# Both halves of a group's scores in one two-bank PSUM tile with a single exponential, in a one-token attention and MLP block

## The chip, the cores and the metric

The kernel runs on one core of a Trainium2 chip. A core has a matrix engine (TensorE, PE in the rows; its weight loads are PEld), a vector engine (VectorE, DVE), a scalar engine (ScalarE, ACT), GpSimd (POOL), and a queue processor (SyncE, SP) that issues the transfers from memory (DMA). TensorE writes only to PSUM, an accumulator of eight banks; a bank holds 512 fp32 columns in each of the 128 partitions. The working memory is SBUF. The metric is device microseconds of one execution, as the median of several. All data here is fp32.

## What is computed

One new token for each of four sequences passes through an attention over the last 1024 cached positions (8 groups of key and value heads, two query heads each) and then through an MLP, both behind a layer norm and with a residual:

```python
B, Sq, D = 4, 1, 448;  Hq, Hkv, Sk, Dh = 16, 8, 4096, 256
W = min(4096, max(256, Sk // 4))                     # 1024 positions
q = (x @ wq).reshape(B, Sq, Hq, Dh).transpose(0, 2, 1, 3)
k = jnp.repeat(k_cache[:, :, Sk - W:, :], rep, axis=1)
v = jnp.repeat(v_cache[:, :, Sk - W:, :], rep, axis=1)
scores = jnp.einsum("bhqd,bhkd->bhqk", q, k) * (Dh ** -0.5)
o = jnp.einsum("bhqk,bhkd->bhqd", softmax(scores), v)
...                                                   # o @ wo, back to (B, 1, D)
x = A_x
h = x + A(layernorm(x), A_k_cache, A_v_cache, A_wq, A_wo)
h2 = h + B(layernorm(h), B_w1, B_b1, B_w2, B_b2)      # B: layernorm, gelu(y @ w1 + b1) @ w2 + b2
```

Each input is read once: 88 MB of keys, values and weights, nearly all of it caches.

## The kernel before

**Groups.** The 8 groups of key and value heads (g = 0 to 7) are worked one after another. For one group the kernel projects the query (`project_q`, L149), multiplies it with the keys (`scores_half`, L168, once for each 512 of the 1024 positions), forms the softmax (`softmax`, L180), transposes the probabilities (`transpose_p`, L200), multiplies them with the values (`values`, L213), scales and transposes the result (`transposed_output`, L231) and multiplies it with the group's output weights into one accumulator (`add_output`, L243); the last two together are `finish` (L298). The steps of neighbouring groups are interleaved: while group g+1 has its scores formed, the values of group g are used.

**Transfers.** Keys, values and weights come in large packed transfers, one after another on SyncE's single queue (`load`, L54). They land in a ring of three SBUF slots of 15,872 columns (`slot`, L51). A transfer into a slot can only be issued when the last reader of what lay there before is done, for most slots the output product of a `finish`. The order is t0 (first weights and the keys of group 0), then twice ta, tb, tc and td (L302 to L332, for g = 0 and g = 3), then te0, te1 and te2 (L336 to L343), which hold the keys of group 7, the values and output weights of groups 6 and 7, and the MLP's weights `w1` and `w2`. The slots te are filled in pieces. Of `w2`, which is used last, pieces of 8, 3, 2 and 1 chunks come in this order.

**One group's softmax.** The two halves of the scores are two PSUM tiles of one bank each, from a pool with two buffers (`ps_s`, L43). After each half VectorE takes the row maximum over 512 columns (L177). Then two small VectorE operations form the larger of the two maxima and multiply it with minus the scale (L183 and L184), ScalarE runs one exponential for each half with that as its bias (L188), each with its own row sum, and VectorE adds the two sums and takes the reciprocal (L193, L194). `transpose_p` has TensorE transpose four blocks of 128 columns for each half (L204); the first four read only the first half of the probabilities. In groups 3 and 6 the two halves of the keys come in different transfers (tc and td), and other work lies between the two halves (L318 to L326). In the other six groups the 16 matmuls of both halves follow each other directly (`scores`, L197).

**Order.** The order of TensorE, ScalarE and SyncE is the order of the program text; VectorE's and GpSimd's are set by a scheduler that puts in the waits too. Every engine works strictly in its order.

**The end.** After group 7's scores (L344) TensorE runs two matmuls whose result is not used (`fill`, L353), transposes group 7's probabilities, and goes on with the values of groups 6 and 7 and the MLP. Short matmuls on a zero tile (`keep_warm`, L349) stand in the gaps. The first eight chunks of `w2` are multiplied at L469, the others at L479, and the result is added at L485 and written out. Two other tiles come from the pool `ps_s`: `last` (L372) for the attention's output and `pu` (L430) for the MLP's first product.

**Rows at the start.** The token and the two biases are turned into rows by six transposes (L289), and ScalarE copies them from PSUM (L291).

Of the kernel before, what the change touches and what calls it, by code (L numbers as in the profile page):

```python
# [20 lines left out]
P = 128  # L21
# [4 lines left out]
FQ = F // 4  # L26
Q = 32
# [6 lines left out]
SCALE = DH ** -0.5  # L34

@with_exitstack
def block_kernel(ctx: ExitStack, tc, wq0, k0, wq1, la, lb, lc, ld, k7, vo, w1, w2, out):
    nc = tc.nc
    const = ctx.enter_context(tc.tile_pool(name="const", bufs=1))
    ring = ctx.enter_context(tc.tile_pool(name="ring", bufs=3))  # L40
    work = ctx.enter_context(tc.tile_pool(name="work", bufs=2))
    once = ctx.enter_context(tc.tile_pool(name="once", bufs=1))
    ps_s = ctx.enter_context(tc.tile_pool(name="ps_s", bufs=2, space=PSUM))  # L43
    ps_t = ctx.enter_context(tc.tile_pool(name="ps_t", bufs=2, space=PSUM))
    ps_o = ctx.enter_context(tc.tile_pool(name="ps_o", bufs=1, space=PSUM))
    ps_m = ctx.enter_context(tc.tile_pool(name="ps_m", bufs=2, space=PSUM))
# [32 lines left out]
    def keys(t):  # L79
        return t.rearrange("p (c b k) -> p c b k", c=2, b=B)  # L80
# [35 lines left out]
    qT = [const.tile([P, 2, B, Q], F32, name=f"qT{i}") for i in range(2)]  # L116
# [48 lines left out]
        for i in range(2):  # L165
            nc.vector.tensor_copy(qT[g % 2][:, :, :, i * REP : (i + 1) * REP], src)

    def scores_half(g, h, kt):  # L168
        s = ps_s.tile([P, 512], F32, tag="s", name=f"s{g}_{h}")
        for c in range(2):  # L170
            for b in range(B):
                nc.tensor.matmul(  # L172
                    s[b * Q : (b + 1) * Q, :], qT[g % 2][:, c, b, :], kt[:, c, b, :],
                    start=(c == 0), stop=(c == 1),
                )
        m = work.tile([P, 1], F32, tag=f"mx{h}", name=f"mx{g}_{h}")
        nc.vector.reduce_max(m, s, axis=AX.X)  # L177
        return s, m

    def softmax(g, parts):  # L180
        halves, mx = zip(*parts)
        nm = work.tile([P, 1], F32, tag="nm", name=f"nm{g}")
        nc.vector.tensor_max(nm, mx[0], mx[1])  # L183
        nc.vector.tensor_scalar_mul(nm, nm, -SCALE)  # L184
        p = once.tile([P, 2 * 512], F32, tag="p", name=f"p{g}")
        sums = work.tile([P, 2], F32, tag="sums", name=f"sums{g}")
        for h in range(2):
            nc.scalar.activation(  # L188
                p[:, h * 512 : (h + 1) * 512], halves[h], AF.Exp, bias=nm, scale=SCALE,
                accum_out=sums[:, h : h + 1],  # L190
            )
        rec = work.tile([P, 1], F32, tag=f"rec{g % 3}", name=f"rec{g}")
        nc.vector.tensor_add(rec, sums[:, 0:1], sums[:, 1:2])  # L193
        nc.vector.reciprocal(rec, rec)  # L194
        return p, rec

    def scores(g, kt):  # L197
        return [scores_half(g, h, kt[h]) for h in range(2)]

    def transpose_p(g, p):  # L200
        for h in range(2):
# [84 lines left out]
    for at, n in ((0, 2), (2 * P, 4)):  # L286
        pr = ps_t.tile([P, n, P], F32, tag="t", name=f"pr{n}")
        for i in range(n):
            nc.tensor.transpose(pr[:, i, :], wide[:, at // P + i].rearrange("p j q -> p (j q)"), ident)  # L289
        cols = min(n * P, rs.shape[1] - at)  # L290
        nc.scalar.copy(rs[:, at : at + cols], pr.rearrange("p i c -> p (i c)")[:, :cols])  # L291

    parts = scores(0, [keys(ka), keys(kb)])
    project_q(1, wq_parts(wqt1, wq1_last))
# [7 lines left out]
    for g in (0, 3):  # L302
        ka, kb, wqt, va = cut(load(slot(f"ta{g}"), 0, la[g // 3]), (HALF, HALF, WEIGHTS, HALF))
        parts = scores(g + 1, [keys(ka), keys(kb)])
        project_q(g + 2, wq_parts(wqt))
        p, rec_next = softmax(g + 1, parts)
        transpose_p(g + 1, p)
        po = po_tile(g)
        va = chunks(va)
        values(g, va, po, range(0, 2))  # L310

        vb, wot, ka, kb = cut(load(slot(f"tb{g}"), 0, lb[g // 3]), (HALF, WEIGHTS, HALF, HALF))
        values(g, va + chunks(vb), po, range(2, 4))
# [8 lines left out]
        first_half = scores_half(g + 3, 0, keys(ka))  # L322
# [3 lines left out]
        parts = [first_half, scores_half(g + 3, 1, keys(kb))]  # L326
        project_q(g + 4, wq_parts(wqt))
        p, rec = softmax(g + 3, parts)
# [40 lines left out]

    keep_warm(2, warm)  # L370
    values(g + 1, vt_last, po_last, range(0, 3))
    last = ps_s.tile([P, 512], F32, tag="s", name="last")[:, :P]  # L372
    ph = last.rearrange("p (i c) -> p i c", i=2)
    add_quadrants(ph, accs, True)
    values(g + 1, vt_last, po_last, range(3, 4))
# [181 lines left out]
```

## Time and profile before

| | |
|---|---|
| median of 3 runs | 213.93 us (213.82 to 213.99) |
| the profiled execution | 214.16 us, of which its span is 212.4 us |
| busy share of the span | PE 63%, PEld 23%, DVE 18%, ACT 10%, POOL 2% |
| the transfer queue's packets | 96.9% of 16 DMA engines over the span, 88.30 MB |
| mean rate over the span | 416 GB/s |
| granted TensorE clock, mean | 0.854 |

The span runs from the first to the last instruction of the profiled execution; the other 1.76 us of its time lie around it. No engine is busy for more than two thirds of the span, while the DMA engines are busy nearly all of it. The row of the granted clock on the page alternates between full and half speed:

```profile
PEclk9999995995896559589969759856985999999999
DMA  7999898999999999999999999999989999999991
```

A digit is a fortieth of the span, 5.3 us; under PEclk it is the clock in tenths, under DMA the busy share in tenths. Up to the thirty-first slice the clock falls to half again and again; after that it stays full.

### The profile page before, as it was taken

The numbers are of one execution on the slowest core, as the hardware profiler recorded it, in microseconds if no ns is written. First come the engines' busy times: TensorE is split into PE (matmuls) and PEld (weight loads), VectorE is DVE, ScalarE is ACT, GpSimd is POOL, SyncE is SP. The second block draws the span as 40 slices with busy tenths as digits, with TensorE's granted clock in tenths as the row PEclk, the third lists the DMA queues.
The fourth block names the chain that finished last, engine by engine and source line by source line (L and its number), as shares of the span: only waits on it lengthen the run. The fifth ranks groups of instructions, "written<-read, shape, count | busy, mean of one in ns | idle before, by whom it ended". The sixth has DMA issues, their size and how long they took to land.

```text
span 212.4 us, 2302 instructions
## 1 busy us (share of the span) xinstructions
PE 133.9 (63%) x976; PEld 48.3 (23%) x976; DVE 39.0 (18%) x170; ACT 22.1 (10%) x54; POOL 5.0 (2%) x16
## 2 busy tenths in 40 slices
PE   0469805843950696288398098138708879978984
PEld 0342201310220221022123023013202323224432
DVE  1520300410230003022013013100301223112310
ACT  2011300300020100030003002001000302010311
POOL 5100000000000000000000000000000000000200
PEclk9999995995896559589969759856985999999999
DMA  7999898999999999999999999999989999999991
GB/s 294 425 396 534 361 488 361 491 394 475 407 395 529 395 407 430 451 403 459 424 424 488 403 395 505 395 430 419 478 350 460 430 429 394 440 400 444 419 384 52
DMA packets 3257, 88.43 MB, mean 416 GB/s; under 512 B 368, under 2 KB 624, under 8 KB 1328
## 3 DMA queue, kind: packets, MB, share of 16 engines
q1 hardware_dynamic: 3248, 88.30, 96.9%
q8 instruction: 7, 0.11, 0.2%
q14 instruction: 2, 0.02, 0.0%
HBM read 88.23 MB, written 0.07 MB: 416 GB/s over the span
## 4 chain that ended last, share of the span: by engine, by line
DMA 78%; PE 16%; SPq 2%; DVE 1%; issue 1%; ACT 1%; ACTq 0%
DMA tb<-lb 22%; DMA ta<-la 21%; DMA td<-ld 20%; DMA te<-w 14%; PE s L172 6%; PE po L216 4%; SPq L58 2%; PE ppt L204 1%; PE pq L152 1%; PE acc L245 1%; PE pa L469 1%; PE py L479 1%; SPq L265 1%; PE pqt L158 1%; ACT qs L154 1%
## 5 line engine op out<-in xcount | busy, mean ns | idle before, releaser
L177 DVE TENSOR_REDUCE mx<-s 128x1 f32<-128x512 f32 x16 | 11.1, 691 | 57.8 <-PE s L172 57.8
L172 PE MATMUL s<-ta,qT 128*32 128x512 f32 x64 | 10.7, 831 | 10.3 <-DMA ta<-la 10.3
L154 ACT COPY qs<-pq 128x512 f32<-128x512 f32 x8 | 4.7, 585 | 113.3 <-PE pq L152 113.3
L188 ACT ACTIVATE p<-s,nm 128x512 f32<-128x512 f32 x16 | 10.9, 687 | 46.1 <-DVE nm L184 46.1
L233 DVE TENSOR_SCALAR o<-po,rec 128x512 f32<-128x512 f32 x8 | 6.0, 750 | 48.5 <-PE po L216 48.5
L216 PE MATMUL po<-tb,pT 128*32 128x512 f32 x32 | 7.2, 1051 | 12.2 <-DMA tb<-lb 12.2
L172 PE MATMUL s<-td,qT 128*32 128x512 f32 x32 | 7.1, 1042 | 12.1 <-DMA td<-ld 12.1
L152 PE MATMUL pq<-tc,yT 128*32 128x512 f32 (+1 forms) x20 | 3.9, 891 | 16.6 <-DMA tc<-lc 16.6
L204 PE MATMUL ppt<-ident,p 128*128 128x128 f32 x64 | 10.5, 287 | 0.7 <-ACT p L188 0.4
L216 PE MATMUL po<-tc,pT 128*32 128x512 f32 x64 | 10.4, 813 | 0.0
L158 PE MATMUL pqt<-ident,qs 128*128 128x128 f32 x32 | 6.6, 341 | 6.0 <-ACT qs L154 6.0
L204 PEld LDWEIGHTS ppt<-ident,p 128*128 128x128 f32 x64 | 6.7, 141 | 6.3 <-ACT p L188 6.3
L160 DVE TENSOR_REDUCE sm<-pqt 128x16 f32<-128x64 f32 x8 | 1.8, 224 | 34.4 <-PE pqt L158 34.4
L216 PE MATMUL po<-te,pT 128*32 128x512 f32 x64 | 7.5, 595 | 0.5 <-DMA te<-vo 0.5
L172 PE MATMUL s<-tb,qT 128*32 128x512 f32 x64 | 7.4, 607 | 0.0
L216 PE MATMUL po<-td,pT 128*32 128x512 f32 x64 | 7.3, 595 | 0.0
L237 PE MATMUL pot<-ident,o 128*128 128x128 f32 x32 | 5.2, 286 | 2.7 <-DVE o L233 2.7
L158 PEld LDWEIGHTS pqt<-ident,qs 128*128 128x128 f32 x32 | 4.2, 169 | 11.4 <-ACT qs L154 9.7
L351 PE MATMUL warm<-idle 128*32 128x512 bf16 x22 | 6.8, 382 | 0.0
L172 PEld LDWEIGHTS s<-ta,qT 128*32 128x32 f32 x64 | 2.6, 148 | 17.7 <-issue 13.7
L208 DVE COPY pT<-ppt 128x16 f32<-128x16 f32 x32 | 4.7, 171 | 7.6 <-PE ppt L204 7.6
L172 PE MATMUL s<-t,qT 128*32 128x512 f32 x32 | 5.4, 833 | 0.5 <-DMA t<-k 0.5
(134 smaller groups left out, 112.4 us busy)
## 6 DMA issues: line engine op xcount, KB each, us to landing
tc<-lc SPq DMA_DIRECT2D x2, 7936.0 KB, 47.0
td<-ld SPq DMA_DIRECT2D x2, 7936.0 KB, 44.0
ta<-la SPq DMA_DIRECT2D x2, 7040.0 KB, 38.1
tb<-lb SPq DMA_DIRECT2D x2, 7040.0 KB, 43.2
te<-vo SPq DMA_DIRECT2D x1, 4992.0 KB, 28.1
t<-k SPq DMA_DIRECT2D x1, 4864.0 KB, 15.8
te<-k SPq DMA_DIRECT2D x1, 4096.0 KB, 37.8
te<-vo SPq DMA_DIRECT2D x1, 3072.0 KB, 14.8
```

What stands on the lines that cost most here:

```text
L152: nc.tensor.matmul(pq[j * Q : (j + 1) * Q, cols], y, w, start=True, stop=True)
L154: nc.scalar.copy(qs, pq)
L158: nc.tensor.transpose(pt[:, i, :], qs[:, i * P : (i + 1) * P], ident)
L172: nc.tensor.matmul(s[b * Q : (b + 1) * Q, :], qT[g % 2][:, c, b, :], kt[:, c, b, :], start=(c == 0), stop=(c == 1),)
L177: nc.vector.reduce_max(m, s, axis=AX.X)
L188: nc.scalar.activation(p[:, h * 512 : (h + 1) * 512], halves[h], AF.Exp, bias=nm, scale=SCALE, accum_out=sums[:, h : h + 1],)
L204: nc.tensor.transpose(pt[:, c, :], p[:, (4 * h + c) * P : (4 * h + c + 1) * P], ident)
L208: nc.vector.tensor_copy(pT[g % 2][:, 2 * h : 2 * h + 2, :, i * REP : (i + 1) * REP], src[:, :, i, :, :REP])
L216: nc.tensor.matmul(po[b * Q : (b + 1) * Q], pT[g % 2][:, c, b, :], vt[c][:, :, b, :], start=(c == 0), stop=(c == NKC // 2 - 1),)
L233: nc.vector.tensor_scalar_mul(o, po, rec)
L237: nc.tensor.transpose(pt[:, i, c], o[:, i, c * P : (c + 1) * P], ident)
L351: nc.tensor.matmul(warm[:Q], idle[:, :Q], idle, start=True, stop=True)
```

## The change

The two halves of a group's scores become one PSUM tile of two banks, from a pool with one buffer instead of two of one bank, so the pool takes as much PSUM as before. The two row maxima go into the two columns of one small tile. One VectorE operation takes the larger of the two columns and multiplies it with minus the scale. One exponential runs over all 1024 columns and leaves the whole row sum, so the addition of two sums goes. The copies of the rows at the start move from ScalarE to VectorE. `last` and `pu` take the first bank of a two-bank tile.

```diff
-    ps_s = ctx.enter_context(tc.tile_pool(name="ps_s", bufs=2, space=PSUM))
+    ps_s = ctx.enter_context(tc.tile_pool(name="ps_s", bufs=1, space=PSUM))
...
-    def scores_half(g, h, kt):
-        s = ps_s.tile([P, 512], F32, tag="s", name=f"s{g}_{h}")
+    def score_tile(g):
+        s = ps_s.tile([P, 2, 512], F32, tag="s", name=f"s{g}")
+        return s, work.tile([P, 2], F32, tag="mx", name=f"mx{g}")
+
+    def scores_half(g, h, kt, part):
+        s, mx = part
         for c in range(2):
             for b in range(B):
                 nc.tensor.matmul(
-                    s[b * Q : (b + 1) * Q, :], qT[g % 2][:, c, b, :], kt[:, c, b, :],
+                    s[b * Q : (b + 1) * Q, h, :], qT[g % 2][:, c, b, :], kt[:, c, b, :],
                     start=(c == 0), stop=(c == 1),
                 )
-        m = work.tile([P, 1], F32, tag=f"mx{h}", name=f"mx{g}_{h}")
-        nc.vector.reduce_max(m, s, axis=AX.X)
-        return s, m
-
-    def softmax(g, parts):
-        halves, mx = zip(*parts)
+        nc.vector.reduce_max(mx[:, h : h + 1], s[:, h, :], axis=AX.X)
+
+    def softmax(g, part):
+        s, mx = part
         nm = work.tile([P, 1], F32, tag="nm", name=f"nm{g}")
-        nc.vector.tensor_max(nm, mx[0], mx[1])
-        nc.vector.tensor_scalar_mul(nm, nm, -SCALE)
+        nc.vector.tensor_scalar(nm, mx[:, 0:1], mx[:, 1:2], -SCALE, op0=ALU.max, op1=ALU.mult)
         p = once.tile([P, 2 * 512], F32, tag="p", name=f"p{g}")
-        sums = work.tile([P, 2], F32, tag="sums", name=f"sums{g}")
-        for h in range(2):
-            nc.scalar.activation(
-                p[:, h * 512 : (h + 1) * 512], halves[h], AF.Exp, bias=nm, scale=SCALE,
-                accum_out=sums[:, h : h + 1],
-            )
         rec = work.tile([P, 1], F32, tag=f"rec{g % 3}", name=f"rec{g}")
-        nc.vector.tensor_add(rec, sums[:, 0:1], sums[:, 1:2])
+        nc.scalar.activation(
+            p, s.rearrange("p h k -> p (h k)"), AF.Exp, bias=nm, scale=SCALE, accum_out=rec
+        )
         nc.vector.reciprocal(rec, rec)
         return p, rec
...
-        nc.scalar.copy(rs[:, at : at + cols], pr.rearrange("p i c -> p (i c)")[:, :cols])
+        nc.vector.tensor_copy(rs[:, at : at + cols], pr.rearrange("p i c -> p (i c)")[:, :cols])
...
-    last = ps_s.tile([P, 512], F32, tag="s", name="last")[:, :P]
+    last = ps_s.tile([P, 2, 512], F32, tag="s", name="last")[:, 0, :P]
...
-    pu = ps_s.tile([P, 512], F32, tag="s", name="pu")[:, :FQ]
+    pu = ps_s.tile([P, 2, 512], F32, tag="s", name="pu")[:, 0, :FQ]
```

The callers pass the tile along (`scores` for six groups, the loop over tc and td for groups 3 and 6) and are otherwise as before.

**TensorE, the scores of group 7.** Two pieces of the engine's order show what the text alone does not. Names are the program's tiles: `s` is the scores, `te` a ring slot (here the one with group 7's keys), `qT` the queries, `DVE_49` the count that VectorE's instructions raise, `DMAHW4_49` a transfer's. Before:

```order
L172 MATMUL s_0_835<-te_821,qT_112 32x512 [waits DMAHW4_49]
L172 MATMUL s_0_835<-te_821,qT_112 32x512 x7
L172 MATMUL s_1_846<-te_821,qT_112 32x512 x8
L355 MATMUL warm_867<-te_821,yT 32x512 x2
L204 MATMUL ppt_0_870<-ident,p_860 128x128 [waits Activation_49]
L204 MATMUL ppt_0_870<-ident,p_860 128x128 x3
L204 MATMUL ppt_1_877<-ident,p_860 128x128 [waits Activation_49]
```

With the change:

```order
L176 MATMUL s_793<-te_779,qT_112 32x512 [waits DMAHW4_49]
L176 MATMUL s_793<-te_779,qT_112 32x512 x7
L176 MATMUL s_793<-te_779,qT_112 32x512 [waits DVE_49]
L176 MATMUL s_793<-te_779,qT_112 32x512 x7
L356 MATMUL warm_819<-te_779,yT 32x512 [waits PE_49]
L356 MATMUL warm_819<-te_779,yT 32x512
L204 MATMUL ppt_0_822<-ident,p_815 128x128 [waits Activation_49]
L204 MATMUL ppt_0_822<-ident,p_815 128x128 x3
L204 MATMUL ppt_1_829<-ident,p_815 128x128 x4
```

The first matmul of the second half now waits for VectorE; the count that it waits for is that of the first half's maximum. All of the transposes now wait for one exponential. The same wait stands in groups 0, 1, 2, 4, 5 and 7. In groups 3 and 6, where other work lies between the halves, it does not:

```order
L176 MATMUL s_677<-tc_641,qT_111 32x512 [waits DVE_49]
L176 MATMUL s_677<-tc_641,qT_111 32x512 x7
L237 MATMUL pot_690<-ident,o_688 128x128 [waits DVE_49]
L237 MATMUL pot_690<-ident,o_688 128x128 x3
L245 MATMUL acc<-tc_641,oT_115 32x448 [waits DVE_49]
L245 MATMUL acc<-tc_641,oT_115 32x448 x3
L176 MATMUL s_677<-td_701,qT_111 32x512 [waits DMAHW3_49]
L176 MATMUL s_677<-td_701,qT_111 32x512 x7
```

These rows are group 6 with the change; the second half, from td, waits for its transfer alone.

**VectorE, group 0.** The copies of the rows (`rs`) now stand on VectorE, the first of them ahead of the copies of the queries, `qT`, that group 0's scores read:

```order
L160 TENSOR_REDUCE sm_168<-pqt_163 128x16 [waits PE_49]
L291 COPY rs<-pr_175 128x256 [waits PE_49]
L166 COPY qT_111<-sm_168 128x8x2 [waits DVE_49]
L166 COPY qT_111<-sm_168 128x8x2
L291 COPY rs<-pr_179 128x448 [waits PE_49]
L180 TENSOR_REDUCE mx_186<-s_185 128x1 [waits PE_49] x2
```

Before, the first copy of `qT` followed the reduction `sm` directly, and both copies of the rows stood on ScalarE between two copies of L154.

More of the change, by code (lines that the diff above doesn't have):

```diff
@@ L197, in scores @@
     def scores(g, kt):
-        return [scores_half(g, h, kt[h]) for h in range(2)]
+        part = score_tile(g)
+        for h in range(2):
+            scores_half(g, h, kt[h], part)
+        return part
     def transpose_p(g, p):
@@ L321, in block_kernel @@
         values(g + 1, chunks(v), po)
-        first_half = scores_half(g + 3, 0, keys(ka))
+        part = score_tile(g + 3)
+        scores_half(g + 3, 0, keys(ka), part)
         finish(g + 1, po, rec_next, wot)
         kb, wqt, v, wot = cut(load(slot(f"td{g}"), 0, ld[g // 3]), (HALF, WEIGHTS, CACHE, WEIGHTS))
-        parts = [first_half, scores_half(g + 3, 1, keys(kb))]
+        scores_half(g + 3, 1, keys(kb), part)
         project_q(g + 4, wq_parts(wqt))
-        p, rec = softmax(g + 3, parts)
+        p, rec = softmax(g + 3, part)
         transpose_p(g + 3, p)
```

## Prediction

> **What bounds the kernel now.** I read the page's chain of waits first, then the transfer queue, then the waits, and last the timeline of the final 50 us.
>
> ```profile
> DMA 78%; PE 16%; SPq 2%; DVE 1%; issue 1%; ACT 1%; ACTq 0%
> q1 hardware_dynamic: 3248, 88.30, 96.9%
> PE pq L152 <- DMA tc<-lc: 16.6, 2, 8.5
> PE po L216 <- DMA tb<-lb: 12.2, 2, 6.4
> PE s L172 <- DMA td<-ld: 12.1, 2, 6.7
> PE s L172 <- DMA ta<-la: 10.3, 2, 7.1
> ```
>
> The first row is the chain by engine: transfers make 78% of it. The second says that the queue's packets fill 96.9% of the DMA engines. The other four are waits (sum, times, longest): TensorE stands idle before every big transfer, and the shortest of these eight waits is 10.3 − 7.1 = 3.2 us. So up to td's second landing each stage starts with a landing, and what a stage computes late ends in that idle time, as long as it is below 3.2 us and the next transfer is still asked for early enough. The place where asking is tightest is te's:
>
> ```profile
> 174.13 1.28 SPq L58 DMA_DIRECT2D te<-vo  x3
> 181.70 0.19 PEld L216 LDWEIGHTS po<-te,pT 128*32 128x32 f32 x8 [0.75 <-PE warm L351]
> 181.73 3.64 PE L216 MATMUL po<-te,pT 128*32 128x512 f32 x32 [0.28 <-DMA te<-vo]
> 160.10 3.64 PE L172 MATMUL s<-td,qT 128*32 128x512 f32 x16 [6.71 <-DMA td<-ld]
> ```
>
> (start and duration in us, and in brackets the idle time and what ended it.) The second piece of `vo` is asked for at 174.13, while the first lands only just before 181.73: 7.5 us in hand. So the stream's end doesn't move with a delay of a microsecond or two. From 160.10, td's last landing, it is different: TensorE computes on to the end with four short waits for transfers, and that stretch, the tail, is where this change can be felt. I call a wait there slack: a delay is eaten by it.
>
> **Part 1: the exponential of group 6**, in the tail.
>
> ```profile
> 165.38 0.69 ACT L188 ACTIVATE p<-s,nm 128x512 f32<-128x512 f32 x1
> 165.96 0.20 ACT L188 ACTIVATION_READ_ACCUMULATOR p<-s,nm 128x1 f32 x1
> 166.21 0.42 PEld L204 LDWEIGHTS ppt<-ident,p 128*128 128x128 f32 x4 [0.26 <-ACT p L188]
> 166.22 1.32 PE L204 MATMUL ppt<-ident,p 128*128 128x128 f32 x8
> L188 ACT ACTIVATE p<-s,nm 128x512 f32<-128x512 f32 x16 | 10.9, 687 | 46.1 <-DVE nm L184 46.1
> L154 ACT COPY qs<-pq 128x512 f32<-128x512 f32 x8 | 4.7, 585 | 113.3 <-PE pq L152 113.3
> L291 ACT COPY rs<-pr 128x256 f32<-128x256 f32 x1 | 0.4, 372 | 1.7 <-PE pr L289 1.7
> ```
>
> The first transposes start 0.83 us after the first exponential (166.21 − 165.38), while the second is still running, and all eight then take 1.32 us without a gap. No row has a pass of 1024 columns. ScalarE's copies give the price of a column: (585 − 372)/256 = 0.83 ns, so 512 more cost 0.43 us, and one exponential is 0.69 + 0.43 = 1.11 us, against two that take 1.36 us. ScalarE gains 0.25 us and TensorE loses 0.43 us, since its first transposes wait for the whole row. The bounds are 0 (columns free) and 0.69 (a second pass as long as the first); I take 0.43, the row of columns. The start of the exponential stays, as it stands behind the copy L154. All after it on TensorE is +0.43.
>
> **Part 2: the scores of group 7.** The piece of TensorE's order for this place shows the added wait: the second half's first matmul waits until VectorE has read the first half. Behind it on TensorE stands the rest of the kernel.
>
> ```profile
> 173.88 3.62 PE L172 MATMUL s<-te,qT 128*32 128x512 f32 x32
> 175.85 0.69 DVE L177 TENSOR_REDUCE mx<-s 128x1 f32<-128x512 f32 x1 [2.80 <-PE s L172]
> 177.57 0.69 DVE L177 TENSOR_REDUCE mx<-s 128x1 f32<-128x512 f32 x1 [1.03 <-PE s L172]
> 178.29 0.16 DVE L183 TENSOR_TENSOR nm<-mx,mx 128x1 f32<-128x1 f32 x1
> 178.49 0.15 DVE L184 TENSOR_SCALAR nm<-nm 128x1 f32<-128x1 f32 x1
> 178.75 0.69 ACT L188 ACTIVATE p<-s,nm 128x512 f32<-128x512 f32 x1 [11.93 <-DVE nm L184]
> 179.58 0.42 PEld L204 LDWEIGHTS ppt<-ident,p 128*128 128x128 f32 x4 [1.30 <-ACT p L188]
> 172.88 0.17 DVE L241 TENSOR_TENSOR oT<-oT,pot 128x16 f32<-128x16 f32 x1
> 173.11 0.16 PEld L245 LDWEIGHTS acc<-td,oT 128*32 128x32 f32 x8 [0.71 <-DVE oT L241]
> ```
>
> The second half's matmuls last half of the 32, from about 175.60 (the next operation follows them at 177.32, and half of 3.44 us is 1.72). The maximum of the first half ends at 175.85 + 0.69 = 176.54. TensorE follows VectorE by 173.11 − 173.05 = 0.06 us, so it goes on at 176.60 to 176.63: a stall of 1.03 us. Below it the bound is the 0.69 us of the maximum alone, above it 1.2 us, if the 0.16 us of weight loads are not hidden either. The one small operation in place of two takes 178.49 − 178.29 = 0.20 us off the path. The exponential then brings its 0.43 us again. The transposes of group 7 come later by 0.43 (part 1) + 1.03 − 0.20 + 0.43 = 1.69 us. The `fill` matmuls, which end at 179.20 now, end 1.46 us later and still before them.
>
> **Part 3: the slack.** Three more rows show the waits for transfers that follow:
>
> ```profile
> 180.84 0.61 PE L351 MATMUL warm<-idle 128*32 128x512 bf16 x2
> 188.94 2.78 PE L216 MATMUL po<-te,pT 128*32 128x512 f32 x24 [0.20 <-DMA te<-vo]
> 206.00 1.71 PE L469 MATMUL pa<-te,gT 128*32 128x448 f32 x16 [0.69 <-DMA te<-w]
> 209.20 0.11 PEld L479 LDWEIGHTS py<-te,gT 128*4 128x4 f32 x8 [0.23 <-DMA te<-w]
> ```
>
> At 181.70 the matmuls would have been free at 180.84 + 0.61 + 0.06 = 181.51, which leaves 0.19; the next two waits are 0.20 and 0.69; at the last the weights wait 0.23 us, of which I count half, 0.11, because matmuls still run. Together 1.19 us. Between these places TensorE, VectorE and ScalarE follow each other without another wait for a transfer. So the end moves by 1.69 − 1.19 = 0.50 us.
>
> **Part 4: what costs nothing.** In groups 0, 1, 2, 4 and 5 the same stall (about 1.0 us) and the late transposes (0.43 us) add at most 1.5 us to a stage, and the smallest idle time of 3.2 us hides it; without that cover each would cost its 1.5 us, 7 us in all. The copies of the rows on VectorE stand ahead of the queries of group 0:
>
> ```profile
> 15.65 0.25 DVE L166 COPY qT<-sm 128x16 f32<-128x16 f32 x2
> 15.82 0.37 ACT L291 COPY rs<-pr 128x256 f32<-128x256 f32 x1 [1.69 <-PE pr L289]
> 17.14 1.08 PE L172 MATMUL s<-t,qT 128*32 128x512 f32 x4 [0.50 <-DMA t<-k]
> ```
>
> VectorE's copy can start at 15.82 like ScalarE's; priced at the 0.69 us of its 512-column row it is over at 16.51 at the latest, and the queries at 16.76, before the keys land at 17.14. The second copy (448 columns, at most 0.69 us) ends long before the first maximum. Without that cover it would cost 0.9 us. The reciprocal, now ahead of the copies behind the transposes, waits for the exponential, which they need too: nothing. The single buffer of `ps_s` adds nothing: the exponential precedes the next scores in TensorE's order by way of the transposes, and `pu` needs what is computed from `last`.
>
> **Part 5: the clock, which can move the tail either way.** The tail starts cold at 160.10. Rows of 2 us, with TensorE's busy time first and the granted clock after the five engines:
>
> ```profile
> 88.00:90.00 2.00, 0.85 (x4) 0.20 (x8) 0.00 (x0) 0.00 (x0) 0.00 (x0) 0.50 1.04 451
> 92.00:94.00 2.00, 1.49 (x14) 0.34 (x6) 1.00 (x3) 0.42 (x1) 0.00 (x0) 0.92 1.04 451
> 140.00:142.00 2.00, 0.66 (x5) 0.38 (x9) 0.00 (x0) 0.00 (x0) 0.00 (x0) 0.50 1.03 444
> 146.00:148.00 2.00, 2.00 (x20) 0.53 (x16) 0.00 (x0) 0.00 (x0) 0.00 (x0) 0.76 1.10 476
> 162.00:164.00 2.00, 2.00 (x17) 0.44 (x10) 0.19 (x1) 0.00 (x0) 0.00 (x0) 0.50 0.84 360
> 99.16:102.57 3.41, 2.06 (x20) 0.57 (x12) 1.10 (x3) 0.00 (x0) 0.00 (x0) 1.00 1.10 467
> ```
>
> Work starts as long before a row's end as TensorE is busy in it, and the mean clock of a row gives the step to full within it (0.92 is a step 0.32 us into the row, 0.76 one 0.96 us into it). So full clock came 3.2 us after the start at 89.15, 5.6 us after that at 141.34 (a gap lies in it) and no sooner than 3.9 us after 160.10. Work at full clock takes half the time, so a step at 3.2 us would bring the tail (3.9 − 3.2)/2 = 0.35 us forward. With no step before the projection is done, its matmuls and the scores' take 5.15 us (3.44 and two passes of a quarter of that) instead of 3.9 + (5.15 − 3.9)/2 = 4.53: 0.62 us later. The kernel before hides either under its slack; the changed one has used that up. I take the middle, (0.62 − 0.35)/2 = 0.13 us. The sum is 0.50 + 0.13 = 0.63 us on a profiled 214.16 us (span 212.4), and set on the median of 213.93 us it gives 214.56, **214.6 us**.
>
> The Trainium skill ("TensorE: Matmul & The Clock Gate", section "What's actually happening") has the clock follow a free-running window of 3413 ns, so that the step falls differently from run to run. The steps here, 3.2 to 5.6 us after the start, agree with that; by the page an estimate of the latest step is two windows, 6.8 us, which would put the tail at the late end above.
>
> **The rivals.** *Late clock:* the step comes after the projection. Price 0.50 + 0.62 = 1.12 us: 215.05 us. For it speaks the stage at 141.34; against it that there a gap broke the work, which the tail doesn't have. *Absorbed:* an early step (−0.35) leaves 0.50 − 0.35 = 0.15 us: 214.1 us, no change that can be told; a stall at its lower bound (0.34 us less) brings 214.2 us without the clock. For it speaks that slack and delay lie within half a microsecond of each other; against it that it needs a cost at its lower end. *Faster:* TensorE's weights at 209.20 already wait for the last transfer, so no gain on an engine can bring the end forward; only the stream can. The rows of 2 us have pieces at 360 GB/s and less instead of 450, each of which costs about 0.4 us; if the changed work kept TensorE and VectorE off the memories during three of these, td would land 1.2 us before 160.1, the tail would start with it, and 214.6 − 1.2 = 213.4 us results. It decides from 1.1 us of earlier landing on; against it, the packets' 96.9% don't depend on what the engines do in any row I found. *Clock lost:* the stall cools the clock, and one stretch of 3.4 us runs at half: 1.7 us, 216.3 us. Against it, the row at 99.16, with TensorE busy for 2.06 of 3.41 us, kept full clock, and the stall leaves 3.41 − 1.03 = 2.4 us in its stretch.
>
> **The numbers.** The forecast 0.50, late clock 0.18, absorbed 0.22, faster 0.06, clock lost 0.04. The likeliest is 214.6; its own range, from the bounds of stall and columns shared out, is 214.2 to 215.0. The whole range reaches down to the absorbed case (213.9 allows for its spread) and up to the late clock (215.3); out of it lie faster, clock lost and a little of each side. A median of this kernel can be told from another by 0.2%, 0.43 us: above 214.36 is slower, which is the forecast less a small part, the late clock and the clock lost, 0.70; the same 0.23; faster 0.07.
>
> **What would show it.** Right: an idle time of about 1.0 us on TensorE within the scores of six groups, ended by the maximum; exponentials of 1.11 us, eight of them; group 7's transposes at about 181.3, if td lands at 160.1; no wait for a transfer left at the values of groups 6 and 7 and at L470. Wrong: a wait of TensorE at L470 that is still there (the tail had more slack than I found), transfers that land at other times, or an exponential whose first transposes start before its end.

## The result and the profile after

| | before | changed |
|---|---|---|
| median | 213.92 us (213.82 to 214.07, 6 runs) | 214.7 us (214.3 to 214.99, 6 runs) |
| ratio, with its 95% interval | | 1.0038 (1.0028 to 1.0048) |
| span, median | 212.1 us (211.9 to 212.4) | 212.75 us (212.3 to 213.1) |
| time outside the span, median | 1.81 us | 1.98 us |
| the profiled execution | 214.16 us, span 212.4 | 214.99 us, span 213.1 |

The changed kernel is slower by 0.78 us, and the table splits that: 0.65 us lie in the span, some 0.15 us outside it. (The spans of the kernel before are those of 35 executions beside the first experiments.) Both profiled executions stand at the upper end of their kernels' spans, so they may be compared with each other.

The page of the changed kernel: its span, the chain of waits by engine, the transfer queue, two waits (sum, times, longest), and the group of the exponential (busy time and mean ns, then the idle time ahead and what ended it):

```profile
span 213.1 us, 2268 instructions
DMA 62%; PE 27%; DVE 4%; ACT 2%; issue 1%; SPq 1%; ACTq 0%; DVEq 0%
q1 hardware_dynamic: 3248, 88.30, 96.6%
PE s L176 <- DVE mx L180: 4.8, 6, 0.8
PE ppt L204 <- ACT p L188: 3.5, 8, 0.7
L188 ACT ACTIVATE p<-s,nm 128x1024 f32<-128x1024 f32 x8 | 8.9, 1117 | 43.1 <-DVE oT L241 29.9 <-DVE nm L185 13.3
```

The stream is the same: 3248 packets, 88.30 MB. The chain holds fewer transfers (62% where it was 78%) and more TensorE (27% where it was 16%). The wait on the maximum is new and there six times, 0.8 us each; the eight exponentials take 1.117 us each; and TensorE now waits ahead of the transposes in all eight groups. Where that costs time is seen in the tail. The timeline of the changed kernel for group 6 (start and duration in us; in brackets the idle time and what ended it):

```profile
160.25 3.64 PE L176 MATMUL s<-td,qT 128*32 128x512 f32 x16 [6.06 <-DMA td<-ld]
166.16 1.12 ACT L188 ACTIVATE p<-s,nm 128x1024 f32<-128x1024 f32 x1
166.32 0.66 PE L158 MATMUL pqt<-ident,qs 128*128 128x128 f32 x4 [0.72 <-ACT qs L154]
167.43 1.09 PE L204 MATMUL ppt<-ident,p 128*128 128x128 f32 x8 [0.45 <-ACT p L188]
168.45 3.64 PE L216 MATMUL po<-td,pT 128*32 128x512 f32 x32
```

and, from the timeline of the kernel before, the place of the queries' transposes:

```profile
165.53 0.66 PE L158 MATMUL pqt<-ident,qs 128*128 128x128 f32 x4 [0.73 <-ACT qs L154]
```

The last transfer td lands 0.15 us later than before (160.25 against 160.10). The queries' transposes come 6.07 us after it, where it was 5.43. The transposes of the probabilities wait for the whole exponential and start 1.11 us after those, where it was 0.69. Group 7 in the same view of the changed kernel:

```profile
174.87 1.90 PE L176 MATMUL s<-te,qT 128*32 128x512 f32 x16
176.84 0.69 DVE L180 TENSOR_REDUCE mx<-s 128x1 f32<-128x512 f32 x1 [2.80 <-PE s L176]
177.58 1.92 PE L176 MATMUL s<-te,qT 128*32 128x512 f32 x16 [0.81 <-DVE mx L180]
180.30 0.21 DVE L185 TENSOR_SCALAR nm<-mx 128x1 f32<-128x1 f32 x1
180.63 1.11 ACT L188 ACTIVATE p<-s,nm 128x1024 f32<-128x1024 f32 x1 [13.26 <-DVE nm L185]
181.89 1.09 PE L204 MATMUL ppt<-ident,p 128*128 128x128 f32 x8 [0.69 <-ACT p L188]
183.57 3.64 PE L216 MATMUL po<-te,pT 128*32 128x512 f32 x32
206.81 1.71 PE L470 MATMUL pa<-te,gT 128*32 128x448 f32 x16
210.36 0.29 DVE L486 TENSOR_TENSOR res<-py,hb 128x128 f32<-128x128 f32 x1 [3.66 <-PE py L480]
```

Between the two halves now stands the first half's maximum (176.84): the second half's matmuls start at 177.58, 2.71 us after the first half's, where 1.72 us would do. The single exponential starts at 180.63. The transposes come at 181.89 (before: 179.58). Neither the values of group 6 (183.57) nor L470 (206.81) waits for a transfer any more: before, both did. The result comes at 210.36, 0.69 us after that of the kernel before:

```profile
209.67 0.29 DVE L485 TENSOR_TENSOR res<-py,hb 128x128 f32<-128x128 f32 x1 [4.42 <-PE py L479]
```

The clock shows in rows of 2 us. Those of the changed kernel (TensorE's busy time first, the granted clock in the third column from the right):

```profile
160.00:162.00 2.00, 1.75 (x12) 0.44 (x16) 0.00 (x0) 0.00 (x0) 0.00 (x0) 0.50 1.03 442
162.00:164.00 2.00, 2.00 (x16) 0.55 (x12) 0.04 (x1) 0.00 (x0) 0.00 (x0) 0.50 0.84 360
164.00:166.00 2.00, 1.60 (x10) 0.35 (x2) 0.86 (x2) 0.32 (x1) 0.00 (x0) 0.63 1.15 483
...
176.00:178.00 2.00, 1.19 (x12) 0.16 (x8) 0.69 (x1) 0.00 (x0) 0.00 (x0) 1.00 0.88 379
```

and the third of these rows for the kernel before:

```profile
164.00:166.00 2.00, 1.27 (x14) 0.64 (x6) 0.81 (x3) 1.10 (x3) 0.00 (x0) 1.00 1.19 500
```

A mean of 0.63 puts the step to full 1.48 us into the row, at 165.5, that is 5.2 us after td's landing. Before it came by 164.0, 3.9 us after it. During the stall (the last row of the changed kernel: TensorE busy for 1.19 of 2 us) the clock stays full.

### The profile page after: what moved, and what is told of

It is laid out like the page before. It is cut to its first block, busy times and chain, and to the rows that moved or that the text cites. A ratio compares the mean times of both kernels' runs of the same rounds, so it can differ in the third digit from the quotient of the medians.

```text
span 213.1 us, 2268 instructions
## 1 busy us (share of the span) xinstructions
PE 134.1 (63%) x976; PEld 48.3 (23%) x976; DVE 38.7 (18%) x156; ACT 19.3 (9%) x36; POOL 5.0 (2%) x16
## 3 DMA queue, kind: packets, MB, share of 16 engines
q1 hardware_dynamic: 3248, 88.30, 96.6%
## 4 chain that ended last, share of the span: by engine, by line
DMA 62%; PE 27%; DVE 4%; ACT 2%; issue 1%; SPq 1%; ACTq 0%; DVEq 0%
DMA tb<-lb 23%; DMA ta<-la 21%; DMA td<-ld 19%; PE s L176 8%; PE po L216 7%; ACT p L188 2%; DVE mx L180 2%; PE pq L152 2%; PE ppt L204 2%; PE pu L444 2%; PE warm L352 1%; PE acc L245 1%; DVE o L233 1%; PE pot L237 1%; PE pa L470 1%
## 5 line engine op out<-in xcount | busy, mean ns | idle before, releaser
L176 PE MATMUL s<-ta,qT 128*32 128x512 f32 x64 | 13.3, 973 | 10.7 <-DMA ta<-la 9.1
L154 ACT COPY qs<-pq 128x512 f32<-128x512 f32 x8 | 4.7, 585 | 122.9 <-PE pq L152 122.9
L188 ACT ACTIVATE p<-s,nm 128x1024 f32<-128x1024 f32 x8 | 8.9, 1117 | 43.1 <-DVE oT L241 29.9
L204 PE MATMUL ppt<-ident,p 128*128 128x128 f32 x64 | 8.7, 279 | 3.5 <-ACT p L188 3.5
L176 PE MATMUL s<-tb,qT 128*32 128x512 f32 x64 | 8.5, 650 | 1.6 <-DVE mx L180 1.6
L216 PE MATMUL po<-tb,pT 128*32 128x512 f32 x32 | 4.8, 721 | 7.2 <-DMA tb<-lb 7.2
L146 POOL TENSOR_TENSOR r<-ve_r,mhalf 128x1 f32<-128x1 f32 x2 | 1.1, 543 | 191.3 <-DVE ve_r L145 191.3
L237 PEld LDWEIGHTS pot<-ident,o 128*128 128x128 f32 x32 | 3.3, 140 | 8.8 <-DVE o L233 7.2
```

The lines of the kernel that those rows point to most:

```text
L154: nc.scalar.copy(qs, pq)
L176: nc.tensor.matmul(s[b * Q : (b + 1) * Q, h, :], qT[g % 2][:, c, b, :], kt[:, c, b, :], start=(c == 0), stop=(c == 1),)
L188: nc.scalar.activation(p, s.rearrange("p h k -> p (h k)"), AF.Exp, bias=nm, scale=SCALE, accum_out=rec)
L204: nc.tensor.transpose(pt[:, c, :], p[:, (4 * h + c) * P : (4 * h + c + 1) * P], ident)
L216: nc.tensor.matmul(po[b * Q : (b + 1) * Q], pT[g % 2][:, c, b, :], vt[c][:, :, b, :], start=(c == 0), stop=(c == NKC // 2 - 1),)
L237: nc.tensor.transpose(pt[:, i, c], o[:, i, c * P : (c + 1) * P], ident)
```

## The experiments

The theory: in groups 0 to 5 nothing is lost; in group 7 the wait for the first half's maximum, and in groups 6 and 7 the late transposes, use up the slack of the tail, and the step of the clock decides how much is left over. The rivals: all six waits cost a little each; the copies on VectorE cost something; the clock suffers from the stall. All times below are medians over several executions, with the range, and each ratio has its 95% interval. The kernel before had 213.91 to 213.92 us beside all of them, at a span of 212.1.

### Without the wait: all groups, and group 7 alone

The edit for group 7; for all groups both conditions are `True`:

```diff
-        nc.vector.reduce_max(mx[:, h : h + 1], s[:, h, :], axis=AX.X)
+        if h == 1 or not (g == HKV - 1):
+            nc.vector.reduce_max(mx[:, h : h + 1], s[:, h, :], axis=AX.X)
...
-        nc.vector.tensor_scalar(nm, mx[:, 0:1], mx[:, 1:2], -SCALE, op0=ALU.max, op1=ALU.mult)
+        lo = 1 if g == HKV - 1 else 0
+        nc.vector.tensor_scalar(nm, mx[:, lo : lo + 1], mx[:, 1:2], -SCALE, op0=ALU.max, op1=ALU.mult)
```

> The maximum over the first half's 512 columns is left out in all groups, so nothing reads the tile between the halves and TensorE has no wait there; the single exponential stays. The theory: 1.0 us of the tail's delay goes, and the end is back at the last transfer: 213.9 to 214.0 us, the idle time within the scores is gone. Rival (the exponential): 214.6 us or more.

> The first half's maximum is left out in group 7 alone; the wait stays in groups 0, 1, 2, 4 and 5. The theory (the five earlier waits end in TensorE's idle time before the next landing): as with the wait gone everywhere, 213.9 to 214.0 us. Rival (the earlier waits cost, about 0.2 us each, by later requests or later clock steps): 214.5 us or more.

All groups: 214.13 us (213.93 to 214.28), 1.0009 (1.0001 to 1.0018), span 212.1. Group 7 alone: 214.01 us (213.81 to 214.12), 1.0004 (0.9996 to 1.0013), span 212.1. Both have the span of the kernel before, so of the six waits only group 7's costs anything in the span, and the other five are hidden. The timeline of the first of the two:

```profile
160.10 3.64 PE L176 MATMUL s<-td,qT 128*32 128x512 f32 x16 [6.01 <-DMA td<-ld]
166.17 0.66 PE L158 MATMUL pqt<-ident,qs 128*128 128x128 f32 x4 [0.72 <-ACT qs L154]
174.72 3.62 PE L176 MATMUL s<-te,qT 128*32 128x512 f32 x32
182.40 3.64 PE L218 MATMUL po<-te,pT 128*32 128x512 f32 x32
209.26 0.29 DVE L488 TENSOR_TENSOR res<-py,hb 128x128 f32<-128x128 f32 x1 [3.73 <-PE py L482]
```

The 32 matmuls run through (174.72), and the values of group 6 come at 182.40 instead of 183.57. The clock was as late here as in the changed kernel (166.17 is 6.07 us after 160.10), and the result still comes at 209.26: a late clock and the late transposes together, without the wait, find enough slack.

### Two exponentials on the two-bank tile

```diff
-        nc.scalar.activation(
-            p, s.rearrange("p h k -> p (h k)"), AF.Exp, bias=nm, scale=SCALE, accum_out=rec
-        )
+        sums = work.tile([P, 2], F32, tag="sums", name=f"sums{g}")
+        for h in range(2):
+            nc.scalar.activation(
+                p[:, h * 512 : (h + 1) * 512], s[:, h, :], AF.Exp, bias=nm, scale=SCALE,
+                accum_out=sums[:, h : h + 1],
+            )
+        nc.vector.tensor_add(rec, sums[:, 0:1], sums[:, 1:2])
```

> Two exponentials of 512 columns over the two-bank tile, as before the change; the added wait stays. The theory (the added wait of about 1.0 us in group 7 is the main term, and the late transposes cost 0.42 us less the 0.23 us by which eight transposes in one stream are shorter, in groups 6 and 7): 0.38 us less than the changed kernel, 214.3 us. Rival (the single exponential is the main term): 213.9 us, as before.

214.1 us (213.81 to 214.71), 1.0014 (1.0006 to 1.0023), span 212.3 (212.0 to 212.9). The span falls by 0.45 us against the changed kernel's, though the wait is still there. The timeline of this kernel at group 6 and its values:

```profile
165.36 0.66 PE L158 MATMUL pqt<-ident,qs 128*128 128x128 f32 x4 [0.73 <-ACT qs L154]
166.04 1.32 PE L208 MATMUL ppt<-ident,p 128*128 128x128 f32 x8
167.29 3.64 PE L220 MATMUL po<-td,pT 128*32 128x512 f32 x32
```

From the queries' transposes to the values it is 167.29 − 165.36 = 1.93 us, as before (1.94), against 168.45 − 166.32 = 2.13 us in the changed kernel. In group 7, from the second half's scores to the values of group 6, it is 5.80 us here and 183.57 − 177.58 = 5.99 us in the changed kernel. So the single exponential costs 0.2 us in each of these two groups. It is a smaller term than the wait.

### TensorE kept awake ahead of td's landing

```diff
+        if g == 3:
+            awake = ps_t.tile([P, 512], F32, tag="t", name="awake")
+            for _ in range(20):
+                nc.tensor.matmul(awake[:Q], idle[:, :Q], idle, start=True, stop=True)
```

> The changed kernel with 20 matmuls on the zero tile ahead of td's second landing, in TensorE's idle time, so that the tail starts at full clock; wait and exponential stay. The theory (the clock's step, 5.2 us after the landing in the profile of the changed kernel, takes the slack away that would have hidden the rest): TensorE gains about 2 us, 213.9 us, and the spread of the runs, 0.7 us now, shrinks to 0.3 us. Rival (the clock is a small term, the wait and the exponential alone decide): 214.5 us or more.

214.24 us (213.75 to 215.66), 1.0026 (1.0012 to 1.004), span 212.1 (211.8 to 212.3, and one of 213.7). The timeline:

```profile
160.31 1.92 PE L176 MATMUL s<-td,qT 128*32 128x512 f32 x16 [1.45 <-DMA td<-ld]
163.82 0.66 PE L158 MATMUL pqt<-ident,qs 128*128 128x128 f32 x4 [0.72 <-ACT qs L154]
181.96 3.63 PE L216 MATMUL po<-te,pT 128*32 128x512 f32 x31 [0.94 <-DMA te<-vo]
205.75 1.71 PE L475 MATMUL pa<-te,gT 128*32 128x448 f32 x16 [0.21 <-DMA te<-w]
```

The 16 matmuls take 1.92 us instead of 3.64, the queries' transposes come 3.51 us after the landing instead of 6.07, and the values of group 6 wait 0.94 us for their transfer. So with wait and single exponential in place, a tail at full clock ends with the span of the kernel before. The expected time of 213.9 us and the narrow spread of 0.3 us didn't come: what is added lies outside the span (1.88 to 3.16 us around it) and isn't explained. A single long span like that of 213.7 us was seen once in the kernel before too (213.6 us).

### The rows copied by ScalarE again

```diff
-        nc.vector.tensor_copy(rs[:, at : at + cols], pr.rearrange("p i c -> p (i c)")[:, :cols])
+        nc.scalar.copy(rs[:, at : at + cols], pr.rearrange("p i c -> p (i c)")[:, :cols])
```

> The changed kernel with the rows at the start copied by ScalarE again, the rest of the change as it is. The theory (the copies on VectorE end before the keys of group 0 land, and are paid for by nothing): as the changed kernel, 214.7 us, span 212.3 to 213.1 us. Rival (they delay group 0, its slot and the stream): 214.4 us or less.

214.79 us (214.33 to 215.08), 1.0031 (1.0018 to 1.0044), span 212.85: the same as the changed kernel. The place of the two copies costs nothing that can be told. On VectorE they take, by the groups of the changed kernel,

```profile
L291 DVE COPY rs<-pr 128x448 f32<-128x448 f32 x1 | 0.6, 625 | 0.2 <-PE pr L289 0.2
L291 DVE COPY rs<-pr 128x256 f32<-128x256 f32 x1 | 0.4, 425 | 0.2 <-PE pr L289 0.2
```

that is less than the 0.69 us at which the prediction had priced each.

### One maximum over 1024 columns

```diff
-        nc.vector.reduce_max(mx[:, h : h + 1], s[:, h, :], axis=AX.X)
+        if h == 1:
+            nc.vector.reduce_max(mx[:, 0:1], s.rearrange("p h k -> p (h k)"), axis=AX.X)
...
-        nc.vector.tensor_scalar(nm, mx[:, 0:1], mx[:, 1:2], -SCALE, op0=ALU.max, op1=ALU.mult)
+        nc.vector.tensor_scalar_mul(nm, mx[:, 0:1], -SCALE)
```

> The changed kernel with one maximum over all 1024 columns of the two-bank tile after both halves, in place of one for each half. Nothing reads the tile between the halves, so the wait of 1.0 us goes, and the maximum, 0.69 us for 512 columns, takes about 0.54 us longer at its end. The theory: 0.45 us less delay in the tail than the changed kernel, like the run with two exponentials: span 212.3 us, 214.2 us. Rival (the wait is free, the exponential is what costs): span 212.8 us or more, 214.7 us or more.

214.36 us (214.04 to 214.66), 1.0017 (1.0005 to 1.0028), span 212.4 (212.0 to 212.6).

```profile
174.09 3.62 PE L176 MATMUL s<-te,qT 128*32 128x512 f32 x32
177.77 1.22 DVE L181 TENSOR_REDUCE mx<-s 128x1 f32<-128x1024 f32 x1 [4.51 <-PE s L176]
180.56 1.09 PE L205 MATMUL ppt<-ident,p 128*128 128x128 f32 x8 [1.16 <-ACT p L189]
```

The wait goes, and the longer maximum (1.22 us instead of 0.69) stands on the path instead. From the first scores to the transposes it is 6.47 us, against 7.02 us in the changed kernel (181.89 − 174.87) and 5.70 us before (179.58 − 173.88). Of the 0.55 us gained here 0.35 us reach the span. Of the three forms with one exponential that compute all and add no other work, this is the fastest.

### Time inserted into the kernel before

Matmuls on the zero tile, some 0.215 us each, stand behind group 7's transposes; the edit is that for six, and 9 and 12 were tried too:

```diff
-    keep_warm(2, warm0)
+    keep_warm(2 + 6, warm0)
```

> The kernel before with 6 more matmuls on the zero tile behind group 7's transposes, 6 x 0.215 = 1.29 us of TensorE, which is the delay that the profile of the changed kernel shows at the values of group 6 once the clock's part is taken off. The theory (only the delay of the tail counts, wherever it comes from): the same time as the changed kernel, span 212.3 to 213.1 us, 214.5 us. Rival (the change costs something beyond the tail): span 212.1 us, 213.9 us.

> The kernel before with 9 more matmuls on the zero tile behind group 7's transposes, 1.94 us, between the runs with 6 (span 212.2 us) and 12 (214.1 us). The theory (a fixed slack, then one for one): the line through the run with 12 gives span 213.4 us, and the run with 6 was below it because its clock steps fell early: 213.4 to 213.5 us. Rival (the slack is larger, and the run with 12 has a cost of its own): 212.8 us or less.

> The kernel before with 12 more such matmuls, 2.58 us. The theory: with the slack used up, the second six are paid in full: 1.29 us more than the run with six, span about 214.0 us, 215.8 us. Rival (the slack is larger than 1.3 us): less than 215.3 us.

| inserted | us | ratio | span |
|---|---|---|---|
| 1.29 us | 214.15 (213.78 to 215.52) | 1.0015 (0.9997 to 1.0033) | 212.25 (212.0 to 212.9) |
| 1.94 us | 215.61 (215.11 to 216.43) | 1.0085 (1.0069 to 1.0101) | 213.5 (213.2 to 213.7) |
| 2.58 us | 216.37 (215.42 to 217.1) | 1.0101 (1.0074 to 1.0128) | 214.1 (213.6 to 214.5) |

The first was a miss, 0.35 us below what was expected; the spans of the other two are as expected, while the time of the last is 0.57 us above the expected 215.8 us. A delay of 1.29 us is almost wholly eaten, and from 1.94 us on each microsecond inserted is one lost (0.64 us more brought 0.6). Between the first two lie 1.25 us for 0.65 us of matmuls. Their values of group 6, in the timeline of each (the first row ends where its view ends):

```profile
182.31 3.21 PE L216 MATMUL po<-te,pT 128*32 128x512 f32 x28
```

```profile
183.71 3.64 PE L216 MATMUL po<-te,pT 128*32 128x512 f32 x32
```

They are 1.40 us apart. Of these, 0.75 us stand there already ahead of the inserted matmuls (group 7's transposes come at 179.10 and 179.85), and the clock made it: full 2.7 us after td's landing in the first, 4.4 us in the second. These are single executions; that the clock stood likewise in the others, and so makes the 1.25 us between the medians, isn't shown. Of these three the times in us are larger and wider than their spans say; that lies around the span (up to 3.0 us) and isn't explained, as with the awake kernel.

### Time inserted in the place of the wait

In the kernel before, five matmuls on the zero tile (1.08 us) between the halves of group 7's scores:

```diff
-    p, rec_last = softmax(g + 1, scores(g + 1, kt))
+    parts = [scores_half(g + 1, 0, kt[0])]
+    for _ in range(5):
+        nc.tensor.matmul(warm0[:Q], idle[:, :Q], idle, start=True, stop=True)
+    parts.append(scores_half(g + 1, 1, kt[1]))
+    p, rec_last = softmax(g + 1, parts)
```

> The kernel before with 5 matmuls on the zero tile, 1.08 us, between the two halves of group 7's scores, in the place of the added wait and of its length; nothing else is changed, and TensorE is busy instead of idle. The theory (the wait is worth its length in delay): as the run with two exponentials on the two-bank tile, span 212.3 us, time outside it 1.8 us, 214.1 us. Rival (the idle time itself costs more, by the clock): span 212.1 us, 213.9 us.

214.39 us (213.89 to 215.69), 1.0025 (1.0011 to 1.0039), span 212.4 (212.0 to 212.9): nearly that of the wait with two exponentials (212.3). A busy delay costs what the idle one costs, to 0.1 us in the span, so the wait has no further price of its own, such as a clock that falls during it.

### ScalarE's count of instructions

The changed kernel was 0.1 to 0.2 us slow even where its span was back at 212.1. Single columns copied by ScalarE near the start bring its count back:

```diff
+    spare = once.tile([P, 1], F32, tag="spare", name="spare")
+    for _ in range(18):
+        nc.scalar.copy(spare, mean[:, 0:1])
```

> The changed kernel with 18 copies of one column on ScalarE in its idle time near the start, so that its instruction count is back at that of the kernel before (54). So far the kernels with 52 or 54 instructions on ScalarE have 1.8 us of their time outside the span and those with 36 or 38 have 1.95 us. The theory that the count decides it: 1.8 us again, the span as the changed kernel's (212.3 to 213.1 us), 214.55 us. Rival (the exponential of 1024 columns or something else decides): 1.95 us, 214.7 us.

214.26 us (213.87 to 214.94), 1.0019 (1.0008 to 1.003), span 212.45 (212.0 to 213.2), and 1.79 us outside it, as before the change. The page of this kernel (engines and one queue):

```profile
PE 133.8 (63%) x976; PEld 48.3 (23%) x976; DVE 38.7 (18%) x156; ACT 22.6 (11%) x54; POOL 5.0 (2%) x16
q14 instruction: 2, 0.02, 0.0%
```

and of the changed kernel:

```profile
PE 134.1 (63%) x976; PEld 48.3 (23%) x976; DVE 38.7 (18%) x156; ACT 19.3 (9%) x36; POOL 5.0 (2%) x16
q14 instruction: 1, 0.01, 0.0%
```

With 54 instructions on ScalarE the queue q14 has two packets and 1.79 us lie around the span; with 36 it has one, and 1.98 us lie around it. All kernels without extra matmuls fall on one of the two sides: the two exponentials (52 instructions) on that of 1.80 us, those with one exponential at 1.93 to 2.0 us. The pair shows that 18 more instructions on ScalarE bring the time back; where between 38 and 52 it changes, and whether the packet is the reason, isn't shown. The span of 213.2 in the range shows also that the tail of the changed kernel, with nothing altered in it, ends anywhere between 212.0 and 213.2.

## Why the prediction was right

The forecast was 214.6 us, by 0.63 us in the span, and came out at 214.7 us with 0.65 us in the span. What happens, and where, was right. That the sum came out so near was luck in part: the clock and td's landing cost 0.66 us more than forecast, the transposes and the slack took 0.66 us more off (with the other rows 0.61 us), and the time around the span was left out. Step by step, in the profiled execution:

| term | forecast | measured | from |
|---|---|---|---|
| transposes of group 6 start later | +0.43 | +0.42 | 1.11 − 0.69 |
| all eight transposes in one go, group 6 | none | −0.23 | 168.45 − 167.43 = 1.02, before 167.47 − 166.22 = 1.25 |
| stall within group 7's scores | +1.03 | +0.99 | 2.71 − 1.72 |
| small operations and transposes of group 7 | −0.20 + 0.43 | +0.33 | 181.89 − 177.58 = 4.31, before 179.58 − 175.60 = 3.98 |
| **delay at group 7's transposes, without the clock** | **1.69** | **1.51** | sum of the four |
| all eight transposes in one go, group 7 | none | −0.25 | 183.57 − 181.89 = 1.68, before 181.51 − 179.58 = 1.93 |
| clock | +0.13 | +0.64 | 6.07 − 5.43 |
| landing of td | none | +0.15 | 160.25 − 160.10 |
| **slack** | **−1.19** | **−1.37** | 2.06 ahead of the values of group 6, 0.69 at the result |

(Of the row of the small operations, from the first of them to the exponential it is 180.63 − 180.30 = 0.33 us where it was 178.75 − 178.29 = 0.46, so 0.13 us are saved instead of 0.20: the one operation takes 0.21 us, each of the two had taken some 0.15. From the exponential to the transposes it is 1.26 us where it was 0.83, the 0.43 of the forecast.) All of this is for one execution of each kernel. The median span is 0.35 us below that of the profiled execution (212.75 against 213.1), and how the terms stood there isn't known.

The last line: TensorE is ready for the values of group 6 at 183.57 and was at 181.51, which is 2.06 us, the sum of the rows above it but for the rounding. There it had waited 0.19 us; up to L470 another 1.06 are eaten (206.81 − 206.00 = 0.81 are left), where 0.20 + 0.69 had been counted, and behind it 0.12, where 0.11 had been. What was counted too small is the wait of 0.20 us at 188.94. Before:

```profile
188.14 0.60 PE L351 MATMUL warm<-idle 128*32 128x512 bf16 x2
192.62 0.59 PE L351 MATMUL warm<-idle 128*32 128x512 bf16 x2
```

and in the changed kernel:

```profile
189.99 0.38 PE L352 MATMUL warm<-idle 128*32 128x512 bf16 x1
190.00 0.63 PE L216 MATMUL po<-te,pT 128*32 128x512 f32 x3
194.08 0.59 PE L352 MATMUL warm<-idle 128*32 128x512 bf16 x2
```

The work between the short matmuls takes 4.48 us before and 4.09 us now, so this wait was worth 0.39 us. Its 0.20 us of idle time count from the end of the short matmuls ahead, but without the wait the values start at 190.00, while those still run. (A fifth wait for a transfer, of TensorE's weights at 207.56, wasn't counted at all; from L469 or L470 to there it is 1.56 us before and 1.50 now.)

**What bounds it.** Right. The five waits in groups 0 to 5 cost nothing in the span, as the pair without waits shows, and nor does the move of the copies, as the kernel that undoes it shows. The end is bound by the stream: the versions without the wait in group 7, and that with the clock awake, have a median span of 212.1 like the kernel before, and none is below. The profiles show the slack as a fixed limit. In the five where TensorE waits for no transfer behind the values of group 6 (the changed kernel, those with the rows on ScalarE, with 18 copies, and with 9 and 12 inserted matmuls) these values start at 183.44 or later, and the result comes 26.79 us behind them, as in 210.36 − 183.57. In the eight where they start at 182.40 or earlier, the result comes at 209.26 to 209.67, whenever they started.

**The stall.** Right, at 0.99 us for 1.03. The order of TensorE told it, not the hardware: before, the maximum of the first half ran from 175.85 to 176.54 while TensorE wrote the second half in another bank. The Trainium skill ("PSUM — Partial Sum Buffer", section "PSUM bank collisions raise a hardware error") asks for a guard by bank and quadrant, and says that accesses to different banks run clean; that row agrees. So the wait comes with the program, most likely from one tile being tracked as one, though the two halves are two banks. A version that keeps two tracked halves and one exponential over both wasn't tried.

**The columns.** The size of the exponential was right (1.117 us for 1.11). Mis-sized was what follows: "+0.43" for all that stands behind it on TensorE. The second four transposes had waited for the second exponential; with the whole row there, all eight take 1.09 us instead of 1.32, and about half of the loss comes back. The kernel with two exponentials shows the net price: 0.2 us for a group.

**The clock.** This was the term most off: the middle of the two ends was taken (+0.13), and the profiled execution stood at the late end, at +0.64, the condition of the late-clock rival. The size of that end (0.62) was right. Over the runs the step falls at other places, and the spans of one and the same tail reach from 212.0 to 213.2.

In these profiles, where the step falls is settled before td lands. Two rows of 1 us, of the changed kernel and of the kernel before, while TensorE is idle:

```profile
158.00:159.00 1.00, 0.00 (x0) 0.00 (x0) 0.00 (x0) 0.00 (x0) 0.00 (x0) 0.82 0.84 360
157.00:158.00 1.00, 0.00 (x0) 0.00 (x0) 0.00 (x0) 0.00 (x0) 0.00 (x0) 0.59 0.59 256
```

From these means the clock falls to half at 158.64 and at 157.18, and the step to full (165.48, and 164.02 by a row of 1 us with a mean of 0.99) comes 6.84 us later in both. In all twelve profiles but the awake one it comes 6.82 to 6.84 us after that fall, which lies anywhere from 156.0 to 158.7. Whether the change itself moves the fall isn't shown: the four latest steps (5.0 to 5.4 us after td's landing) are all in kernels with one exponential, but two others with it have theirs at 2.9 and 4.0 us. The Trainium skill ("TensorE: Matmul & The Clock Gate", section "What's actually happening") has the transition depend on where a free-running window stands, which the spread of 2.7 to 5.4 us agrees with; the ±500 ns that it gives for this is smaller than the spread here. With the clock awake the whole loss in the span goes, and without the wait even the late clock is free, in the profile that has it. So it takes the wait and a late clock together to get beyond the slack, and the late transposes add to both.

**The rivals.** *Late clock* had the right place and the right price for its term, but its 215.05 us didn't come, since the delay was 0.4 us smaller than forecast (1.51 − 0.25 = 1.26 against 1.69). *Absorbed* is where some executions come near (214.3 us, span 212.3). *Faster* needed td to land earlier; it landed 0.15 us later. *Clock lost* falls with the busy delay in the place of the wait, and with the clock of 1.00 in the row from 176.00, in which the stall lies.

**What was missing.** The forecast was set on the median as if the time around the span were fixed. It grew by 0.15 us with the fewer instructions on ScalarE, a fifth of the loss.

## What to carry to other kernels

A fusion that saves instructions can still lose: two tiles that become one share their waits, so look in the engine's order for a writer of one half that now waits for a reader of the other, and for a consumer that now waits for the whole. Count slack and delay of such a stretch from the last transfer that starts it, and count the step of the clock as part of the delay, with both ends: where slack and delay lie within a microsecond of each other, the clock decides from run to run. In a kernel bound by its transfers, ask first which stages hide the change: five of the six new waits here cost nothing, and without the sixth the loss in the span is gone.

## What the runs showed of the hardware

- The step to the full clock came 2.7 to 5.4 us after TensorE's work began behind td's landing, in kernels with the same work there. Some half of it reaches the tail: 1.3 us between the kernel before and the changed one brought 0.64 us, 1.7 us between six and nine inserted matmuls 0.75 us.
- The step to the full clock came 6.82 to 6.84 us after the clock had fallen to half, at this place in twelve profiles, whether TensorE's work in between began 1.4 or 4.1 us after the fall.
- Eight transposes of 128x128 in one go take 1.09 us; split by a wait, with the first four early, 1.32 us.
- The time around the span was 1.79 to 1.81 us with 52 to 54 instructions on ScalarE and 1.93 to 2.0 us with 36 to 38.
- Kernels with more than the usual short matmuls on the zero tile had up to 3.16 us around the span in some executions, without a cause that the profile shows.
- An exponential over two PSUM banks took 1.117 us for 1024 columns, where one bank's 512 took 0.687: the second 512 cost 0.43 us, the column price of ScalarE's copies.
